# z turned once per half of the rows, and copied to the other half

## The chip, the cores and the metric

One core of one Trainium2 chip runs the kernel. TensorE (PE) does the matmuls and loads their weights (PEld), VectorE (DVE) and ScalarE (ACT) the elementwise work, GpSimd (POOL) and SyncE (SP) issue most DMAs, and 16 DMA engines move the bytes. The time is device microseconds per execution; the median of the runs counts.

## The reference, cut to what matters

```python
# u, v: (8, 3072, 256); z: (8, 3072, 64); float32
scores = (1 / 3072) * np.matmul(z, z.transpose(0, 2, 1))
attn = np.maximum(scores, 0.0) ** 2
x = (u * np.matmul(attn, v)).reshape(8 * 3072, 256)
g = np.maximum(x @ w1, x @ w2)          # w1, w2: 256 x 1024
out = g @ w_out                         # 1024 x 256
```

An attention without softmax over 8 batches, with the scores z zT, followed by a feed-forward layer on all tokens.

## The kernel before

**Tiles.** The 3072 rows of a batch are 24 tiles of 128 rows. Four tiles make a group (g, 512 columns of scores), six groups a batch; two groups are a couple, written (b, c) for batch b, c = 0 to 2. Eight tiles of z or v make a piece, three to a batch. The data are cast to bf16.

**Scores.** z has only 64 columns, so TensorE's 128 rows are used as two halves of 64: `score_pair` (L230) issues two matmuls (L244), one in each half of the rows, which run side by side; half 0 takes the first tile of the pair and half 1 the second. Each reads 64 x 128 weights and 64 x 512 moving columns from `zT`, which holds z turned (features on partitions) for both halves: rows 0 to 63 and rows 64 to 127. `z_at(b, t, half)` (L111) gives the place of a tile in it. There is room for four pieces; piece number 3b + piece goes to slot (3b + piece) mod 4.

**How z gets there.** For batches 2 to 7 `load_z` (L157) loads a piece in bf16 by a DMA from GpSimd; `turn_z` (L163) makes two VectorE copies (L169) that write every tile twice, side by side, into a tile `zd` of 8 x 2 x 64 columns, and one DMA transpose from SP (L170) turns 128 x 1024 elements, so that each tile stands in both halves of the rows. For batch 1 `z_staged` (L151) loads float32 by SP into a free block and GpSimd casts it twice into `zd`. Batch 0 is turned on TensorE.

**Attention.** Relu of the scores goes to a block (128 x 2048, one of 27 in a list that is handed round), its square stays there. The scores are symmetric, so only blocks on and above the diagonal are computed; `mirror` (L287) makes the others by a DMA transpose of 128 x 2048 from SP (L289), and a diagonal block fills its lower triangle by three small ones (L271). From batch 0's last couple on, the product with v is done with seven products in place of eight on sums of blocks (VectorE, L343) and of v (`combine_v`, L193); the matmuls are L1202, 84 steps of two for a couple of batch 1 or later.

**Feed-forward.** `ff_by_seven` (L527) follows for the couple before, and its four results per couple leave by ScalarE copies (L649) and DMAs from SP (L650).

**The order.** Nothing is reordered: every engine and every DMA queue runs its instructions in the order in which the program is written. `at(n, ...)` puts work ahead of step n of a couple; things of one step go in the order of the `at` calls, after the mirrors that became due. In a pass of the loop over couples come the 84 steps of couple (b, c), with the score pairs of what is computed ahead spread among them (at step 2 + n x 82 // N for the n-th of N), then the loads of `loads_behind`, then the feed-forward of the couple before, its output DMAs included. So on SP's queue the four output stores of one pass stand ahead of everything of the next pass's steps. Pairs run ahead: couple (b, 1) computes the last 6 pairs of batch b and the first 8 of batch b + 1, and couple (b, 2) the next 14.

For batch b + 1 the z pieces 0 and 1 are loaded and turned in couple (b, 0) (turned at steps 62 and 74 for b = 1, 44 and 56 for later b) and piece 2 is turned at step 26 of couple (b, 1). Turns of u (`turn_u`, L218, DMA L220) stand at steps 12 and 18 of the couples (b, 1) and (b, 2).

v is loaded by GpSimd (L186) in DMAs of two tiles, 128 KB each, but for batch 0 where they hold four tiles.

Of the kernel before, what the change touches and what calls it, by code (L numbers as in the profile page):

```python
# [12 lines left out]
def kernel(  # L13
# [10 lines left out]
    nc = tc.nc  # L24
    fp32 = mybir.dt.float32
    bf16 = mybir.dt.bfloat16
# [4 lines left out]
    dqk = z.shape[-1]  # L31
    Dff = moe_w1.shape[-1]

    P = 128
    R = 64
    NT = S // P
    G = 4
    GW = G * P
    NG = NT // G
    NC = NG // 2  # L40
# [10 lines left out]
    zpool = ctx.enter_context(tc.tile_pool(name="zpool", bufs=2))  # L51
# [12 lines left out]
    def by_tile(x):  # L64
        return x.rearrange("(p t) d -> p t d", t=NT)
# [39 lines left out]

    zT = zpool.tile([P, 1 + 4 * 2 * G, P], bf16, name="zT", bufs=1)
    zn, zd, z_first, resting = {}, {}, [], []

    def z_at(b, t, half=0):  # L111
        piece, k = divmod(t, 2 * G)
        return 1 + (NC * b + piece) % 4 * 2 * G + k - (half if b == 0 else 0)

    def first_z(lo, n, queue):
        t = hpool.tile([P, n, dqk], fp32, name=f"z32_{lo}", tag="h")
# [19 lines left out]
    def staged(dst, src):  # L136
        home = Block()
        resting.append(home)
        t = home.ap.bitcast(fp32)[:, : dst.shape[1] * dst.shape[2]]
        t = t.rearrange("p (a f) -> p a f", a=dst.shape[1])  # L140
        nc.sync.dma_start(out=t, in_=src)
        return t

    def rested(n):
        for _ in range(n):
            resting.pop(0).release()
# [2 lines left out]
        nc.gpsimd.tensor_copy(dst, staged(dst, src))  # L149

    def z_staged(b, piece):  # L151
        zd[b, piece] = t = zpool.tile([P, 2 * G, 2, dqk], bf16, name="zd")
        t32 = staged(t[:, :, 0, :], by_tile(z[b])[:, ds(piece * 2 * G, 2 * G), :])
        for h in range(2):
            nc.gpsimd.tensor_copy(t[:, :, h, :], t32)

# [4 lines left out]
        )  # L161

    def turn_z(b, piece):  # L163
        if (b, piece) in zd:
            t = zd[b, piece]
        else:
            t = zpool.tile([P, 2 * G, 2, dqk], bf16, name="zd")
            for h in range(2):
                nc.vector.tensor_copy(t[:, :, h, :], zn[b, piece])  # L169
        nc.sync.dma_start_transpose(  # L170
            zT[:, ds(z_at(b, piece * 2 * G), 2 * G), :], t.rearrange("p t h d -> p (t h d)")
        )

# [2 lines left out]
    def load_v(b, piece, lo=0, n=2 * G, held=False):  # L178
        if (b, piece) not in vp:
            vp[b, piece] = vpool.tile([P, 2 * G, D], bf16, name="v_sb")  # L180
        t = vp[b, piece]
        if held:
            nc.vector.memset(t[:, lo, 0:1], 0.0)
        step = 2 if b else n
        for at in range(lo, lo + n, step):
            nc.gpsimd.dma_start(  # L186
                out=t[:, ds(at, step), :], in_=by_tile(v[b])[:, ds(piece * 2 * G + at, step), :]
            )

    def v_at(b, t, dc):  # L190
# [39 lines left out]
    def score_pair(b, g, m, dve_half=None, halves=False, act=False):  # L230
# [9 lines left out]
        for h in range(2):  # L240
            rows = ds(h * R, R)
            q = z_at(b, g * G, h)
            s_ps.append(mm_tile([P, GW], fp32, "s_ps", full=not lo[h])[0])
            nc.tensor.matmul(  # L244
                s_ps[h][:, lo[h] :],
                zT[rows, z_at(b, blk * G + tiles[h], h), :],
                zT[rows, q + lo[h] // P : q + G, :].rearrange("p t c -> p (t c)"),
                start=True,
                stop=True,
            )  # L250
# [600 lines left out]
    def need(b, g, n):  # L851
        most = pair_at[b, g, 2 * g]
        for t in range(n + 1):
            if t // G >= g:
                most = max(most, pair_at[b, g, t // 2] + 1)
        return most

    with tc.manual_schedule():
# [3 lines left out]
        nc.vector.memset(warm[:, :P], 0.0)  # L862
        nc.vector.memset(warm[:, P:], 0.0)
        load_v(0, 0, 0, G)
        make_identity(nc, ident)
        z32.update({lo: first_z(lo, n, nc.gpsimd) for lo, n in ((12, 8), (20, 4))})
        load_v(0, 0, G, G)
        for piece in range(1, NC):
            for lo in (0, G):
                load_v(0, piece, lo, G)  # L870
# [43 lines left out]
        for i in range(PLAIN):  # L914
            b, g = groups[i]
# [5 lines left out]
            for slot, (n, dc) in enumerate(steps_of(i)):  # L921
                k = need(b, g, n)
# [22 lines left out]
                if i in (1, 2) and n in (6, 9):  # L945
                    h = sums[n // 9]
# [21 lines left out]
                if (i, n) in ((1, 15), (2, 14), (3, 4)):  # L968
                    z_staged(1, i - 1)
# [8 lines left out]
                if (i, n) in ((2, 10), (3, 10)):  # L978
                    turn_z(1, i - 2)
                if (i, n) == (3, 16):  # L980
                    turn_z(1, 2)
# [6 lines left out]
                if i == 2 and n in (15, 18):  # L988
                    half = n // 18
# [67 lines left out]
        b, g = groups[PLAIN - 1]  # L1057
# [14 lines left out]
        for i in range(PLAIN // 2, len(couples)):  # L1072
            b, c = couples[i]
            q1, q2 = 2 * c, 2 * c + 1
            if (b, c) == (1, 0):
# [3 lines left out]
                b, c, forms, blocks=() if b else (q2, q1)  # L1079
# [6 lines left out]
            acc, opened, h = {}, {}, {}  # L1086
# [68 lines left out]
            def at(n, do, *args):  # L1155
                events.setdefault(n, []).append(lambda: do(*args))
# [8 lines left out]
                at(18, turn_u, b, q2)  # L1165
            if not b:
                at(20, lambda: rested(len(resting)))
                for n in range(12):
                    at(
                        12 + 7 * n - n // 3 if n < 8 else 21 + 6 * n,  # L1170
                        load_v, 1, (2, 1, 0)[n // 4], 2 * (n % 4), 2,
                    )
            elif b + 1 < B:
                if c == 0:
                    for piece, n in enumerate((24, 30) if b == 1 else (4, 10)):
                        at(n, load_z, b + 1, piece)
                        at((62 if b == 1 else 44) + 12 * piece, turn_z, b + 1, piece)
                    at(80 if b == 1 else 62, load_z, b + 1, 2)
                if c == 1:
                    for n in range(4):  # L1180
                        at(24 + 5 * n, load_v, b + 1, 1, 2 * n, 2)
                    at(26, turn_z, b + 1, 2)

            for s, pair in enumerate(steps):
                tick += 1
# [106 lines left out]
```

## Time and profile before

| | |
|---|---|
| median of 3 runs | 893.77 us (892.32 to 895.35) |
| the profiled execution, in all | 894.84 us |
| its span, first to last instruction | 892.8 us |
| mean granted TensorE clock | 0.999 |
| DMA queue of SP (q1) | 73.9% of 16 engines |
| DMA queue of GpSimd (q0) | 22.6% of 16 engines |
| HBM read, written | 59.77 MB, 25.17 MB |

The profile is that of one execution, in microseconds from the span's start. A row of instructions names the line, the engine, the operation, what it writes and reads, and how many there are; "SPq" is a row of SyncE's queue, whose length is the time that SP takes to issue it, while the landing of a DMA comes later and is listed apart. A DMA issue row such as this one gives count, size and the median time from issue to landing:

```profile
zT<-zd SPq DMA_TRANSPOSE x21, 4.3
v_sb<-in_v_dram POOLq DMA_DIRECT2D x84, 128.0 KB, 6.6
v_sb<-in_v_dram POOLq DMA_DIRECT2D x6, 256.0 KB, 6.2
```

A wait names who waited and for whom, with the sum in us, the number of times and the longest. The share of the DMA engines in a window can go above 1.0, because the packets of one engine overlap.

### The profile page before, as it was taken

The page shows a single profiled execution, that of the slowest core. Times are in us where ns is not written, and L with a number is a line of the kernel's source. Part 1 is how long each engine was busy: PE and PEld are TensorE (multiplying, and loading weights), DVE is VectorE, ACT ScalarE, POOL GpSimd, SP SyncE. Part 2 cuts the span into 40 slices and gives each one's busy share as a digit, 9 for nine tenths or more (in the row PEclk, how much of TensorE's full clock was granted, in tenths as well). Part 3 has the DMA queues.
Part 4 walks back from the last instruction along what each step waited for, and adds up shares of the span by engine and source line. Part 5 has one row for each costly group of instructions (what it writes and reads, how often), then busy time and mean ns, then how long its engine had stood idle before and what let it go on. Part 6 is the DMA issues. An engine that isn't in the chain of part 4 may idle for free.

```text
span 892.8 us, 19566 instructions
## 1 busy us (share of the span) xinstructions
PE 885.2 (99%) x7458; PEld 505.5 (57%) x7458; DVE 764.9 (86%) x1201; ACT 735.4 (82%) x1366; POOL 97.7 (11%) x176
## 2 busy tenths in 40 slices
PE   9999999999999999999999999999999999999997
PEld 4555555565565555655656556566465564655655
DVE  6897887889988899798998899988898889987755
ACT  7978888788888888888888889888889888894554
POOL 3222100111002010020101101011100110000000
PEclk9999999999999999999999999999999999999999
DMA  9999999989899889998999999999989999998302
GB/s 179 250 224 197 201 198 146 205 145 197 168 178 185 175 139 161 191 151 165 173 168 203 153 183 160 149 198 134 212 150 144 189 134 205 144 150 158 80 1 95
DMA packets 396014, 148.10 MB, mean 166 GB/s; under 512 B 361264, under 2 KB 375856, under 8 KB 395920
## 3 DMA queue, kind: packets, MB, share of 16 engines
q1 hardware_dynamic: 373488, 119.32, 73.9%
q0 software_dynamic: 22288, 27.40, 22.6%
q8 instruction: 58, 0.95, 0.4%
q14 instruction: 36, 0.29, 0.1%
q10 hardware_dynamic: 144, 0.13, 0.0%
HBM read 59.77 MB, written 25.17 MB: 95 GB/s over the span
## 4 chain that ended last, share of the span: by engine, by line
PE 98%; DVE 1%; DMA 1%; issue 0%; ACT 0%; DVEq 0%
PE acc L1202 45%; PE acc L552 21%; PE d_ps L607 11%; PE s_ps L244 7%; PE acc L305 4%; PE d_ps L569 4%; PE acc L733 2%; PE d_ps L711 2%; DMA blk<-blk 1%; PE acc L892 0%; PE tpz L129 0%; DVE h_sb L1097 0%; PE w2o_ps L1000 0%; PE acc L675 0%; DVE blk L268 0%
## 5 line engine op out<-in xcount | busy, mean ns | idle before, releaser
L1202 PE MATMUL acc<-blk,v_sb 64*128 64x512 bf16 x2144 | 386.9, 376 | 0.0
L258 ACT ACTIVATE blk<-s_ps 128x512 bf16<-128x512 f32 (+1 forms) x584 | 287.4, 554 | 62.9 <-PE s_ps L244 60.5
L343 DVE TENSOR_TENSOR blk<-blk,blk 128x2048 bf16<-128x2048 bf16 x260 | 313.0, 1220 | 18.4 <-DMA blk<-blk 11.4
L1202 PE MATMUL acc<-blk,vt 64*128 64x512 bf16 x1560 | 316.3, 376 | 0.0
L1202 PEld LDWEIGHTS <-v_sb 64*128 64x128 bf16 x2144 | 152.0, 94 | 126.0 <-issue 5.0
L552 PE MATMUL acc<-w_out_sb,g_sb 128*128 128x256 bf16 x1400 | 190.3, 273 | 0.0
L552 PEld LDWEIGHTS <-g_sb 128*128 128x128 bf16 x1400 | 136.9, 98 | 56.1 <-DVE g_sb L619 0.6
L1202 PEld LDWEIGHTS <-vt 64*128 64x128 bf16 x1560 | 123.8, 94 | 75.5
L582 ACT ACTIVATE g_sb<-d_ps 128x512 bf16<-128x512 f32 x212 | 120.1, 600 | 9.0 <-PE d_ps L607 7.8
L244 PE MATMUL s_ps<-zT 64*128 64x512 bf16 (+3 forms) x672 | 125.5, 357 | 0.5 <-DVE r_sb L256 0.3
L619 DVE CUSTOM_DVE_ANT_0 g_sb<-blk,d_ps 128x512 bf16<-128x512 f32 x133 | 88.7, 684 | 36.4 <-PE d_ps L607 23.7
L268 DVE TENSOR_TENSOR blk<-blk 128x1024 bf16<-128x1024 bf16 x134 | 89.2, 686 | 19.9 <-ACT blk L258 19.9
L266 ACT ACTIVATE blk<-blk 128x1024 bf16<-128x1024 bf16 x78 | 82.3, 1055 | 0.9
L615 ACT COPY blk<-d_ps 128x512 f32<-128x512 f32 x133 | 76.6, 588 | 6.7 <-PE d_ps L607 3.7
L1097 DVE TENSOR_TENSOR h_sb<-h_sb,acc 128x512 f32<-128x512 f32 x89 | 58.9, 684 | 24.0 <-PE acc L1202 16.0
L186 POOL DMA_DIRECT2D v_sb<-in_v_dram x90 | 48.5, 557 | 272.6 <-PE acc L1202 216.5
L607 PE MATMUL d_ps<-blk,wT_sb 128*128 128x512 bf16 x198 | 68.4, 379 | 0.3 <-DVE g_sb L619 0.3
L473 DVE SCALAR_TENSOR_TENSOR xT<-h_sb,uT 128x512 bf16<-128x512 f32 x96 | 61.3, 689 | 2.1 <-DMA uT<-un 2.1
L649 ACT COPY o_sb<-acc 128x512 f32<-128x512 f32 x86 | 48.2, 587 | 14.5 <-PE acc L552 12.0
L244 PEld LDWEIGHTS <-zT 64*128 64x128 bf16 x672 | 35.7, 94 | 37.6 <-issue 0.4
L1101 ACT COPY h_sb<-acc 128x512 f32<-128x512 f32 x66 | 38.9, 590 | 19.3 <-PE acc L1202 17.8
L611 ACT COPY d_ps<-d_ps 128x512 f32<-128x512 f32 x65 | 37.8, 581 | 16.9 <-PE d_ps L607 16.9
(91 smaller groups left out, 782.4 us busy)
## 6 DMA issues: line engine op xcount, KB each, us to landing
out_dram<-o_sb SPq DMA_DIRECT2D x95, 256.0 KB, 3.0
un<-in_u_dram POOLq DMA_DIRECT2D x44, 256.0 KB, 5.3
v_sb<-in_v_dram POOLq DMA_DIRECT2D x84, 128.0 KB, 6.6
blk<-blk SPq DMA_TRANSPOSE x240, 5.1
zn<-in_z_dram POOLq DMA_DIRECT2D x18, 128.0 KB, 4.7
blk<-in_u_dram SPq DMA_DIRECT2D x4, 512.0 KB, 4.5
v_sb<-in_v_dram POOLq DMA_DIRECT2D x6, 256.0 KB, 6.2
blk<-in_moe_w_dram SPq DMA_DIRECT2D x2, 512.0 KB, 4.3
```

The costliest lines, as they stand in the source:

```text
L244: nc.tensor.matmul(s_ps[h][:, lo[h] :], zT[rows, z_at(b, blk * G + tiles[h], h), :], zT[rows, q + lo[h] // P : q + G, :].rearrange("p t c ...
L258: nc.scalar.activation(o, s, AF.Relu)
L266: nc.scalar.activation(both, r, AF.Square)
L268: nc.vector.tensor_mul(both, r, r)
L343: op(*((by_key(x) if mixed else x.ap) for x in blocks))
L473: lambda dc=dc: nc.vector.scalar_tensor_tensor(out=x[:, dc, :].rearrange("p (t r) -> p t r", r=P), in0=hs[dc].rearrange("p (t r) -> p t r" ...
L552: nc.tensor.matmul(o_ps[key][:, t % 2, :], x[:, ts(t, P)], w, start=first, stop=not left[key] and t % 2 == 1, skip_group_check=last,)
L582: nc.scalar.activation(g, ps, AF.Relu)
L607: nc.tensor.matmul(ps, w, x, start=first, stop=ends, skip_group_check=True)
L615: nc.scalar.copy(u_[k, name], ps)
L619: nc.vector._custom_dve(TENSOR_ADD_SAT, out=g, in0=u_[k, with_], in1=ps, s0=float("inf"), s1=0.0)
L1202: mm = nc.tensor.matmul(a.out(acc[name]), w()[rows], a.moving(rows, j), start=first, stop=left[name] == 0, skip_group_check=True,)
```

## The change

Four things change.

- z of batches 2 to 7 is turned once. One VectorE copy makes a tile `zp` of four column groups, each with a tile of the piece's first half (tiles 0 to 3) beside one of its second half (4 to 7), and a DMA transpose of 128 x 512 puts the first four in rows 0 to 63 and the last four in rows 64 to 127. `spread_z` then issues two plain DMAs from SP, each of 64 partitions x 4 tiles (1 KB per partition, 64 KB), that copy to each half the tiles that the other has: one from rows 64 to 127 to rows 0 to 63 four tiles on, one from rows 0 to 63 to rows 64 to 127 four tiles before. `zT` gets 40 tile places in place of 33, and `z_at` moves accordingly.
- The places of `spread_z` in the order: for batches 3 to 7 at steps 64 and 76 of couple (b, 0) for pieces 0 and 1; for batch 2 at steps 6 and 14 of couple (1, 1); piece 2 of each of these batches at step 48 of couple (b, 1).
- z of batch 1 is still turned twice over, but GpSimd casts it into the second half of the block that the load landed in, and these three blocks go back to the list at step 4 of couple (0, 2).
- v of batches 1 to 7 is loaded in DMAs of four tiles (256 KB) in place of two.

```diff
-    zT = zpool.tile([P, 1 + 4 * 2 * G, P], bf16, name="zT", bufs=1)
-    zn, zd, z_first, resting = {}, {}, [], []
+    zT = zpool.tile([P, 5 * 2 * G, P], bf16, name="zT", bufs=1)
+    zn, zd, z_first, z_homes, resting = {}, {}, [], [], []

     def z_at(b, t, half=0):
+        if b == 0:
+            return 1 + t - half
         piece, k = divmod(t, 2 * G)
-        return 1 + (NC * b + piece) % 4 * 2 * G + k - (half if b == 0 else 0)
+        slot = (NC * b + piece) % 4
+        return G * (1 + 2 * slot + slot // 2) + k - (G * half if b > 1 else 0)
...
     def z_staged(b, piece):
-        zd[b, piece] = t = zpool.tile([P, 2 * G, 2, dqk], bf16, name="zd")
-        t32 = staged(t[:, :, 0, :], by_tile(z[b])[:, ds(piece * 2 * G, 2 * G), :])
+        width = 2 * G * 2 * dqk
+        t32 = staged(zT[:, : 2 * G, :dqk], by_tile(z[b])[:, ds(piece * 2 * G, 2 * G), :])
+        z_homes.append(resting.pop())
+        t = z_homes[-1].ap[:, width : 2 * width].rearrange("p (t h d) -> p t h d", h=2, d=dqk)
+        zd[b, piece] = t
...
     def turn_z(b, piece):
+        at = z_at(b, piece * 2 * G)
         if (b, piece) in zd:
             t = zd[b, piece]
         else:
-            t = zpool.tile([P, 2 * G, 2, dqk], bf16, name="zd")
-            for h in range(2):
-                nc.vector.tensor_copy(t[:, :, h, :], zn[b, piece])
+            t = zpool.tile([P, G, 2, dqk], bf16, name="zp")
+            nc.vector.tensor_copy(
+                t, zn[b, piece].rearrange("p (h t) d -> p t h d", h=2)
+            )
         nc.sync.dma_start_transpose(
-            zT[:, ds(z_at(b, piece * 2 * G), 2 * G), :], t.rearrange("p t h d -> p (t h d)")
+            zT[:, ds(at, t.shape[1]), :], t.rearrange("p t h d -> p (t h d)")
         )
+
+    def spread_z(b, piece):
+        at = z_at(b, piece * 2 * G)
+        lo, hi = (zT[ds(h * R, R), ds(at, G), :] for h in range(2))
+        nc.sync.dma_start(out=zT[ds(0, R), ds(at + G, G), :], in_=hi)
+        nc.sync.dma_start(out=zT[ds(R, R), ds(at - G, G), :], in_=lo)
...
-        step = 2 if b else n
-        for at in range(lo, lo + n, step):
+        for at in range(lo, lo + n, G):
             nc.gpsimd.dma_start(
-                out=t[:, ds(at, step), :], in_=by_tile(v[b])[:, ds(piece * 2 * G + at, step), :]
+                out=t[:, ds(at, G), :], in_=by_tile(v[b])[:, ds(piece * 2 * G + at, G), :]
             )
...
                 at(20, lambda: rested(len(resting)))
-                for n in range(12):
-                    at(
-                        12 + 7 * n - n // 3 if n < 8 else 21 + 6 * n,
-                        load_v, 1, (2, 1, 0)[n // 4], 2 * (n % 4), 2,
-                    )
+                at(4, lambda: [home.release() for home in z_homes])
+                for n, step in enumerate((12, 26, 39, 52, 69, 81)):
+                    at(step, load_v, 1, (2, 1, 0)[n // 2], G * (n % 2), G)
             elif b + 1 < B:
                 if c == 0:
                     for piece, n in enumerate((24, 30) if b == 1 else (4, 10)):
                         at(n, load_z, b + 1, piece)
                         at((62 if b == 1 else 44) + 12 * piece, turn_z, b + 1, piece)
+                        if b > 1:
+                            at(64 + 12 * piece, spread_z, b + 1, piece)
                     at(80 if b == 1 else 62, load_z, b + 1, 2)
                 if c == 1:
-                    for n in range(4):
-                        at(24 + 5 * n, load_v, b + 1, 1, 2 * n, 2)
+                    for n in range(2):
+                        at(24 + 10 * n, load_v, b + 1, 1, G * n, G)
                     at(26, turn_z, b + 1, 2)
+                    at(48, spread_z, b + 1, 2)
+                    if b == 1:
+                        for piece in range(2):
+                            at(6 + 8 * piece, spread_z, b + 1, piece)
```

## The prediction

> **What bounds the kernel now.** I read the page first, parts 1 and 4.
>
> ```profile
> span 892.8 us, 19566 instructions
> PE 885.2 (99%) x7458; PEld 505.5 (57%) x7458; DVE 764.9 (86%) x1201; ACT 735.4 (82%) x1366; POOL 97.7 (11%) x176
> ...
> PE 98%; DVE 1%; DMA 1%; issue 0%; ACT 0%; DVEq 0%
> ```
>
> TensorE is busy for 885.2 of 892.8 us and holds 98% of the chain that ended last. Work saved on another engine shows only where TensorE waits for it. So the second view is TensorE's own waits from 60 us to the end:
>
> ```profile
> PE d_ps L607 <- DVE g_sb L619: 1.5, 2, 1.2
> PE s_ps L244 <- DVE r_sb L256: 0.3, 1, 0.3
> ```
>
> That is all that a faster VectorE or a freer DMA could give back: 1.8 us. The 1.5 us sit at 147 to 151 us, where VectorE waited for a mirrored block that landed late (in the chain, "DMA blk<-blk" for 4.83 us from 141.94).
>
> The change lives on SP's queue and the DMA engines, so the third view is SP's timeline in the couple (1,1):
>
> ```profile
> 148.10 1.85 SPq L170 DMA_TRANSPOSE zT<-zd  x1
> ...
> 155.24 1.29 SPq L170 DMA_TRANSPOSE zT<-zd  x1
> 156.62 1.28 SPq L220 DMA_TRANSPOSE uT<-un  x1
> 158.00 4.80 SPq L289 DMA_TRANSPOSE blk<-blk  x1
> 162.90 2.09 SPq L650 DMA_DIRECT2D out_dram<-o_sb  x4
> 165.09 2.60 SPq L220 DMA_TRANSPOSE uT<-un  x1
> 167.86 5.34 SPq L289 DMA_TRANSPOSE blk<-blk  x1
> 173.29 1.26 SPq L220 DMA_TRANSPOSE uT<-un  x1
> ```
>
> Each row starts where the one before ends: SP has no idle time here and runs behind. How far behind is seen from the data of the four output stores: ScalarE wrote the last of it at 156.21 + 1.24 = 157.45 us, and SP issues the first store at 162.90.
>
> **The change, part by part.**
>
> *z of batches 3 to 7 (and piece 2 of batch 2).* Per piece, one VectorE copy instead of two: the row L169 has 286 ns for a 512-column copy, so 18 x 0.29 = 5.1 us less VectorE. Worth nothing: TensorE's only waits for VectorE are the two above, which lie before all but three of these copies. On SP the turn halves to 512 columns, but the issue hardly does: L170 takes 1.287 us for 1024 columns, L271 1.201 us for 384 to 128, so 0.09 us saved. Two copies are added. No SBUF to SBUF copy is in the trace; the nearest rows are the output stores L650, 0.406 us of issue each, or 2.09 / 4 = 0.52 with the gaps. Per piece SP is busy 2 x 0.52 - 0.09 = 0.95 us longer, 2.9 us per batch of some 108 us. SP waits on many rows and catches up in every stretch of the feed-forward, so I cost this at nothing; without that cover the blocks behind it come 0.95 us later per piece. The tightest of these pieces is piece 2 of batch 4: the slot of its copies is at 399.0 us, just ahead of a mirror, they land at 406 to 408, and TensorE's first use is at 409.2. That holds, with 1 to 3 us to spare. For pieces 0 and 1 of batch 3 (slots at 256.7 and at latest 266.4, uses at 273.85 and 282.4) there are some 10 us. Each copy also waits on SP for its turn to have landed (median 4.3 us after issue). Twenty steps lie between, over 4 us, and the turn itself is ahead in the same queue, so this wait is nothing while SP lags; without the lag, 1 us of SP time, which then has room.
>
> *v loads.* Outside batch 0, 84 loads of 128 KB become 42 of 256 KB. GpSimd saves 42 x 0.557 = 23.4 us of issue that nobody waits for. Landing: 6.6 us for 128 KB, 6.2 for 256 KB, so no later. Nothing; the cover is the feed-forward that follows, and without it half a microsecond per batch either way.
>
> *The blocks that hold z of batch 1.* GpSimd casts into the second half of the staging block, and three blocks of 27 go back at step 4 of the couple (0,2): two of them later than before, one earlier than step 20. No instruction is added. I cost it at nothing, with the 1.8 us of TensorE's known waits as its bound above and below, since it can only move mirrors of that stretch.
>
> *z of batch 2, pieces 0 and 1: the price.* Here the copies are put at steps 6 and 14 of the couple (1,1). In SP's order step 6 stands behind the four stores L650 and ahead of turn_u of step 12, which is the row at 165.09. Step 14 stands behind the mirror of step 13, ahead of the row at 173.29. When does TensorE need them? The couple has 14 score pairs (28 matmuls L244), the n-th at step 2 + n x 82 // 14; the first six finish batch 1, the seventh, at step 37, is batch 2's first. It needs both copies, since each half of the rows reads the other's tiles. In TensorE's timeline the seventh stands here, and the thirteenth, the first with piece 1, below it:
>
> ```profile
> 165.74 0.38 PE L244 MATMUL s_ps<-zT 64*128 64x512 bf16 x2
> ...
> 174.26 0.38 PE L244 MATMUL s_ps<-zT 64*128 64x512 bf16 x2
> ```
>
> So the score matmul that needs the copies comes 0.65 us after SP so much as reaches their slot. Step by step: the slot at 165.09; less what the two halved turns ahead of it give back. SP's issue alone would give 2 x 0.09 = 0.2 us. The DMA engines would give 2 x 0.9: queue q1's 373,488 packets hold 73.9% of 16 engines for 892.8 us, 28 ns each, and 512 of them over 16 engines are 0.9 us. The engines are full here (share 1.16 from 143 to 160 us), so I take 1.3. First copy at 163.8, second at 163.8 + 0.52 = 164.3. Its landing goes by the rows that stand directly ahead of it in the queue:
>
> ```profile
> out_dram<-o_sb SPq DMA_DIRECT2D x4, 256.0 KB, 5.6
> ...
> blk<-blk SPq DMA_TRANSPOSE x2, 8.0
> ```
>
> (the window 156 to 172 us). From below: 2.0, the fastest L650 of the kernel; from above: 8.0, the mirrors of this window. I take 5.6, as the copy queues behind those very stores: 169.9. TensorE then stands still from 165.74 to 169.9, **4.2 us**. Queued behind that matmul is all of TensorE's program; ScalarE and VectorE wait for it and nothing runs on, so it is added whole. The second piece: slot 173.29 - 1.3 + 0.52 x 2 = 173.0 for the first copy, 173.5 for the second, landed some 5 us later (uT's turns, its neighbours there, take 4.0 over the kernel and 5.8 in that window), at 178.5. Needed at 174.26 + 4.2 = 178.5, so it adds about nothing; alone it would cost as much as the first.
>
> The Trainium skill, "DMA: Bandwidth & Descriptors", section "Anatomy of one DMA — SWDGE (gpsimd) path", gives a DMA about 2.0 us plus its bytes at 436 GB/s; it fits that on GpSimd's path. For a 64 KB copy that is an estimated 2.15 us, and the sum would come to 0.7 us of waiting. No trace so far shows such a copy; the L650 rows of this window, 5.6 us, are above that figure.
>
> **Sum.** 892.8 + 4.2 = 897.0 us of span. That execution took 894.84 in all, 1.07 above the median of the runs, 893.77; on the median the forecast is 893.77 + 4.2 = **898.0 us**.
>
> **Rivals.**
> 1. *SP has caught up (not slower).* If the slow stretch of DMA at 159 to 161 us (63, 38 and 21 GB/s in the window's slices) does not recur, the stores go out at 157.5, as their data come, take 2.09, and the copies follow at 159.6 and 160.1. They land 3.0 to 5.6 us later, by 165.7, and TensorE waits for nothing. It decides once SP reaches the slot before 165.74 - 5.6 - 0.52 = 159.6. For it: the runs differ by 3 us, so such stretches come and go. Against: SP's rows have no gap from 143 us on. Time 893.8, or 892.0 with all 1.8 us won back; I write 893.3. Chance 0.25.
> 2. *The copies do not queue.* They land at the 2.0 us of the fastest store: 166.3, a wait of 0.6, 894.4 us. For it: L650's median over the kernel is 3.0, so where nothing is queued a transfer is back soon, and a copy carries a quarter of a store's bytes. Against: the stores just ahead took 5.6. The Trainium skill's figure above would put it here. Chance 0.12.
> 3. *Nothing is given back and both pieces are late.* Copies at 165.1 and 165.6, landed 8.0 later at 173.6: 7.9 us. The second piece from 173.29 + 1.04 + 0.52 = 174.9, landed at 182.9, against 174.26: 8.6 us in all, 902.4. For it: 8.0 is the mirrors' own row in this window. Chance 0.08.
> 4. *The freed DMA time is worth more than the waits show.* Halved turns and longer v packets would have to quicken TensorE itself by over 2.7 us; part 4 shows 98% TensorE and no wait left to fill. 890.5 us. Chance 0.07.
>
> **How the numbers follow.** The forecast has 0.48. About 0.3%, 2.7 us, is what a measurement of this kernel tells from no change. Slower by more: forecast and rival 3, 0.56. Within: rivals 1 and 2, 0.37. Faster: rival 4, 0.07. The forecast's own range runs from a landing of 4.1 us to the full 8.0 without relief, 2.7 to 7.9 us, so 896.5 to 901.7. The range for 8 in 10 goes on to rivals 1 and 2 below (892.0, less 0.3 for the runs' spread, 891.7) and to rival 3 above, 902.4.
>
> **What would show it.** In the profile after: a TensorE wait at L244 for "DMA zT<-zT" near 166 us, about 4 us long, and none like it in batches 3 to 7; SP's copies right behind four L650 rows; L170 at about 1.2 us. Wrong: no such wait (rival 1, if the stores go out by 158; rival 2, if they still go out late), or L244 waiting in later batches, which would say that SP's 2.9 us per batch has no cover.

## The result, and the profile after

The kernel after takes **906.14 us** (median of 5 runs, 904.56 to 908.50) against 893.77 before (5 runs, 892.32 to 897.82). The ratio is 1.0126, with a 95% interval of 1.0097 to 1.0155: 1.3% slower. The forecast was 898.0, the upper end of its range 902.4. Ratios, here and below, leave out executions that took over 1.5% longer than the fastest of the same kernel; medians and ranges are of all. The profiled execution has a span of 904.4 us, 11.6 more than before.

The head of the page and its chain of waits, after:

```profile
span 904.4 us, 19530 instructions
...
PE 889.1 (98%) x7458; PEld 512.3 (57%) x7458; DVE 761.4 (84%) x1183; ACT 736.0 (81%) x1366; POOL 74.9 (8%) x134
...
PE 93%; DMA 4%; DVE 2%; issue 1%; ACT 0%; SPq 0%; DVEq 0%; POOLq 0%
```

Before, TensorE was busy for 885.2 of 892.8 us, so 7.6 idle; now it is 889.1 of 904.4, so 15.3 idle. The 11.6 us are 7.7 more of idle time and 3.9 more of "busy" time for the same 7458 matmuls. The second number can't be a wait: the matmuls themselves have become longer somewhere. DMA has gone from 1% of the chain to 4%.

TensorE's waits after (sum, times, longest):

```profile
PE s_ps L257 <- DMA zT<-zT: 7.3, 1, 7.3
PE acc L1219 <- DVE h_sb L1110: 2.0, 2, 1.4
...
PE acc L1219 <- DVE blk L356: 0.8, 1, 0.8
```

One wait for the copies (L257 is the score matmul, L244 before), a single time, and none in batches 3 to 7. The two lower rows lie between 90 and 140 us; before had none of this size there.

SP's queue around the couple (1,1), after. Start, length of the issue, line (L178 the turn of z, L233 of u, L302 the mirror, L663 the stores, L185 and L186 the copies):

```profile
159.78 1.26 SPq L233 DMA_TRANSPOSE uT<-un  x1
161.14 4.99 SPq L302 DMA_TRANSPOSE blk<-blk  x1
166.22 2.06 SPq L663 DMA_DIRECT2D out_dram<-o_sb  x4
168.33 0.54 SPq L185 DMA_DIRECT2D zT<-zT  x1
168.92 0.58 SPq L186 DMA_DIRECT2D zT<-zT  x1
```

The order is that of before, with the copies directly behind the four stores. The next two views are TensorE's first score matmul of batch 2, with the idle time ahead of it, and the windows before it, during the wait, behind it and after that (length; busy us of PE, PEld, DVE, ACT and POOL; granted clock; DMA share; GB/s):

```profile
175.68 0.86 PE L257 MATMUL s_ps<-zT 64*128 64x512 bf16 x2 [7.28 <-DMA zT<-zT]
```

```profile
160.00:168.00 8.00, 8.00 (x79) 5.16 (x76) 6.24 (x11) 6.54 (x14) 2.11 (x4) 1.00 0.95 156
168.00:175.60 7.60, 0.40 (x4) 0.00 (x0) 3.58 (x8) 0.59 (x1) 0.00 (x0) 0.86 1.12 262
175.60:180.20 4.60, 4.52 (x22) 3.02 (x24) 1.42 (x2) 3.03 (x5) 0.00 (x0) 0.50 0.99 207
180.20:189.00 8.80, 8.80 (x87) 7.29 (x85) 6.22 (x16) 5.38 (x14) 2.12 (x4) 1.00 0.48 80
```

The first copy was issued at 168.33, TensorE stopped at 168.4 (175.68 - 7.28), and the matmul ran at 175.68: from issue to use 7.3 us. Behind the wait the granted clock is 0.50 for 4.6 us, which takes another 4.6 x 0.50 = 2.3 us. A pair of score matmuls shows it too: 0.86 us here, 0.38 before the change. So the one stall costs 7.3 + 2.3 = 9.6 of the 11.6 us; the waits of 2.0 and 0.8 us between 90 and 140 us are the next part, and 1.5 us of before's wait at 147 us are gone.

What stood ahead of the copies shows in the stores' row of the window 156 to 172 us (5.6 before, in the prediction) and in the packets of two stretches, 168.3 to 173.5 and 173.5 to 175.7 us. A copy moves 1 KB packets, a store and a load here 2 KB, a transpose 256 bytes:

```profile
out_dram<-o_sb SPq DMA_DIRECT2D x4, 256.0 KB, 7.3
```

```profile
DMA packets 796, 1.40 MB, mean 269 GB/s; under 512 B 120, under 2 KB 120, under 8 KB 795
...
q0 software_dynamic: 338, 0.59, 65.5%
q1 hardware_dynamic: 457, 0.79, 42.3%
```

```profile
DMA packets 940, 0.55 MB, mean 251 GB/s; under 512 B 685, under 2 KB 813, under 8 KB 940
```

In the first stretch no packet lies between 512 bytes and 2 KB: both copies had been issued by 169.5 us, and until 173.5 none of their packets had started. In the second there are 813 - 685 = 128, all of both copies. So the copies did stand behind the stores in SP's queue for most of their 7 us, and the stores took 7.3 us to land, with GpSimd's loads (q0) holding 65.5% of the engines' time beside them.

Where the loss ends shows in TensorE's rows. Here is the same group near the end, before and then after:

```profile
879.66 0.60 PE L552 MATMUL acc<-w_out_sb,g_sb 128*128 128x256 bf16 x4
```

```profile
891.90 0.60 PE L565 MATMUL acc<-w_out_sb,g_sb 128*128 128x256 bf16 x4
```

TensorE reached batch 2's first score 2.7 us later than before (168.4 against 165.74). At batch 3's first score it is 12.3 us behind (286.17 against 273.85) and here 12.2, so in this execution nothing is lost after the stall.

### The profile page after: what moved, and what is told of

The parts are those of the page before. It is cut to its first block, busy times and chain, and to the rows that moved or that the text cites. A ratio compares the mean times of both kernels' runs of the same rounds, so it can differ in the third digit from the quotient of the medians.

```text
span 904.4 us, 19530 instructions
## 1 busy us (share of the span) xinstructions
PE 889.1 (98%) x7458; PEld 512.3 (57%) x7458; DVE 761.4 (84%) x1183; ACT 736.0 (81%) x1366; POOL 74.9 (8%) x134
## 4 chain that ended last, share of the span: by engine, by line
PE 93%; DMA 4%; DVE 2%; issue 1%; ACT 0%; SPq 0%; DVEq 0%; POOLq 0%
PE acc L1219 43%; PE acc L565 21%; PE d_ps L620 11%; PE s_ps L257 7%; PE acc L318 5%; PE d_ps L582 4%; DMA blk<-blk 2%; PE acc L746 1%; DVE blk L356 1%; DMA zT<-zT 1%; PE d_ps L724 1%; DMA v_sb<-in_v_dram 1%; PE w2o_ps L1013 0%; DVE blk L277 0%; PE acc L688 0%
## 5 line engine op out<-in xcount | busy, mean ns | idle before, releaser
L257 PE MATMUL s_ps<-zT 64*128 64x512 bf16 (+3 forms) x672 | 129.7, 359 | 7.3 <-DMA zT<-zT 7.3
L257 PEld LDWEIGHTS <-zT 64*128 64x128 bf16 x672 | 37.5, 94 | 45.8 <-DMA zT<-zT 7.9
L565 PE MATMUL acc<-W2o_sb,xT 128*128 128x256 bf16 x344 | 51.6, 273 | 0.0
```

The source lines that it names most:

```text
L257: nc.tensor.matmul(s_ps[h][:, lo[h] :], zT[rows, z_at(b, blk * G + tiles[h], h), :], zT[rows, q + lo[h] // P : q + G, :].rearrange("p t c ...
L565: nc.tensor.matmul(o_ps[key][:, t % 2, :], x[:, ts(t, P)], w, start=first, stop=not left[key] and t % 2 == 1, skip_group_check=last,)
```

## The experiments

The runs of before that stand beside the experiments have medians of 894.0 to 895.1 us. Ratios are to these, with 95% intervals. "Steps" are those of the couple.

**1. The copies early.** The kernel after, with the copies of batch 2's pieces 0 and 1 at the end of couple (1,0)'s steps, ahead of the mirror and the stores.

```diff
+            if (b, c) == (1, 0):
+                for piece in range(2):
+                    spread_z(2, piece)
...
-                    if b == 1:
-                        for piece in range(2):
-                            at(6 + 8 * piece, spread_z, b + 1, piece)
```

> The changed kernel, but the copies of batch 2's pieces 0 and 1 stand at the end of couple (1,0)'s steps, ahead of the mirror and the four output stores of that pass. Theory (the copies queue behind the stores): they land by 166 us, the 7.3 us wait of TensorE for zT is gone and the slow pace after it (1.5 us) with it: 906.1 - 8.8 = 897.3. Rival, the wait only moves (stores and mirrors behind them late): over 900.

Measured: **896.50 us** (12 runs, 891.88 to 906.75), 1.0012 [0.999, 1.0035]. TensorE's waits:

```profile
PE acc L565 <- DVE g_sb L632: 5.1, 2, 3.3
PE acc L1216 <- DVE blk L356: 2.7, 1, 2.7
```

No wait for the copies is left; they landed 4.1 to 5.0 us after issue. Moving four instructions gives back some 10 of the 12 us, so the place of these copies is the main loss. The two waits shown are others; the profiled execution was the longest of the twelve, so they speak of its own excess over the median, not of the median.

**2. The copies behind the mirror, ahead of the stores.**

```diff
+                if (b, c) == (0, 2) and token == "E0":
+                    for piece in range(2):
+                        spread_z(2, piece)
```

> The changed kernel, but batch 2's four copies stand behind the mirror and ahead of the four output stores of the same pass: only the order of copies and stores is exchanged. In the profile after, the mirror issued at 161.14 landed at 169.46, the stores from 172.77 to 175.37 and the first two copies at 175.63 and 175.89, one behind the other. Theory, first come first served in SP's queue: the copies land 0.3 to 0.6 us behind the mirror, at about 170, TensorE waits some 2 us, the clock does not drop, and the time is 906.1 - 5.3 - 2.3 = 898.5. Rival, a copy takes 7 us from its issue in this stretch whatever stands ahead of it: landed at 173.3, a wait of 5 us, 903 to 904.

Measured: 901.01 us (10 runs, 892.72 to 903.06), 1.0067 [1.0044, 1.009]. The first row is TensorE's wait; behind it stands SP's queue:

```profile
PE s_ps L257 <- DMA zT<-zT: 4.6, 2, 2.8
```

```profile
159.77 5.14 SPq L302 DMA_TRANSPOSE blk<-blk  x1
165.00 0.55 SPq L185 DMA_DIRECT2D zT<-zT  x1
165.61 0.58 SPq L186 DMA_DIRECT2D zT<-zT  x1
```

The copies are issued 3.3 us earlier than in the kernel after, and the wait shrinks by 2.7 us. But with no store ahead of them they still land 5.2 us (at 170.2) and 6.8 us (at 172.4) after issue, while GpSimd's loads hold 88.9% of the engines' time (165.6 to 170.2 us): taking the stores away does not make the landing short. The clock behind this wait was 0.61 for 4.4 us. The time lies between the expected 898.5 and the rival's 903.

**3. The copies from ScalarE's queue**, at the same steps.

```diff
-                            at(6 + 8 * piece, spread_z, b + 1, piece)
+                            at(6 + 8 * piece, spread_z, b + 1, piece, nc.scalar)
```

> The changed kernel with those four copies issued from ScalarE's queue in place of SP's, at the same steps 6 and 14. If the copies were late because they stood in SP's queue behind a mirror and four stores: issued at about 161 us, landed 2 to 3 us later, no wait, 897.3. If the 16 DMA engines are simply full: landed 5 to 7 us after the issue, by 168, a wait of 0 to 2 us, 897 to 900, and the landing tells it.

Measured: 905.69 us (6 runs, 895.23 to 915.18), 1.0098 [1.006, 1.0136]. ScalarE's timeline, in the longest of these executions:

```profile
157.77 0.51 ACTq L185 DMA_DIRECT2D zT<-zT  x1
...
170.78 0.47 ACTq L185 DMA_DIRECT2D zT<-zT  x1
172.30 0.47 ACTq L186 DMA_DIRECT2D zT<-zT  x1
172.81 1.43 ACT L271 ACTIVATE blk<-s_ps 128x128 bf16<-128x128 f32 x4 [9.21 <-DMA out_dram<-o_sb]
```

The first piece's copies, issued at 157.77 and 160.19 with nothing ahead in their own queue, land at 163.0 and 167.0, after 5.3 and 6.8 us (DMA share 0.89 and 1.09 in these stretches). With run 2 that makes 5 to 7 us for a 64 KB copy from either queue. The run can't price the copies themselves: the second piece's issue was held until 170.8. What held it is open: the view puts ScalarE's 9.2 us of idle time down to SP's stores, whose data these copies neither read nor write. TensorE then waited 7.9 us for ScalarE's relu. In this execution a DMA put on a computing engine's queue held that engine.

**4. TensorE kept busy during the wait.** The kernel after, with 34 matmuls of 128 x 512 ahead of batch 2's first score, into a PSUM bank that this score then overwrites.

```diff
+            if (b, g, m, h) == (2, 0, 2, 0):
+                for _ in range(34):
+                    nc.tensor.matmul(
+                        s_ps[0], w15_sb[:, 0, :P], w15_sb[:, 0, :GW], start=True, stop=True
+                    )
```

> The changed kernel; ahead of batch 2's first score matmul TensorE multiplies 34 times 128x512 (7.3 us at the full clock) into the same bank of PSUM, which the score matmul then starts anew, so the product is thrown away. The wait for the copies is filled with work, nothing else is moved. In the profile after, the granted clock is 0.50 from 175.6 to 180.2 us, right behind 7.3 us of waiting. Theory, the idle time itself drops the clock: the copies land as before, the granted clock stays 1.00 behind them, and the time is 906.1 - 2.3 = 903.8. Rival, the slow stretch has another cause (DMA traffic, weight loads): clock 0.5 there again and 906.1.

Measured: 900.87 us (8 runs), 1.0087 [1.0055, 1.012]. Five of the runs lie at 900.1 to 901.5 and three at 907.3 to 908.7. TensorE's timeline and two windows:

```profile
167.35 7.51 PE L259 MATMUL s_ps<-w_sb 128*128 128x512 bf16 x33
174.79 0.39 PE L262 MATMUL s_ps<-zT 64*128 64x512 bf16 x2
```

```profile
172.00:176.00 4.00, 4.00 (x26) 1.68 (x25) 0.00 (x0) 0.79 (x2) 0.00 (x0) 1.00 1.28 212
176.00:180.00 4.00, 4.00 (x42) 2.14 (x38) 3.63 (x5) 3.75 (x8) 0.00 (x0) 1.00 0.64 127
```

The copies, issued at 166.00 and 166.71, are as late as ever (landed 7.0 and 7.1 us after issue, the last at 173.8), but the clock stays at 1.00 and the pair of scores takes 0.39 us, not 0.86. The score stands right behind the added matmuls, some 1 us after the last copy. So idle time, not the transfers, brought the half clock. What this is worth in time is less clear: the windows give 2.3 us less that 1 us, the medians 5.3 us, but these come from different sets of runs, and the ratios' intervals overlap (1.0087 to 1.0126, or 3.5 us).

**5. v by two tiles in the kernel after**, at the steps of before, everything else as changed.

```diff
-        for at in range(lo, lo + n, G):
+        step = 2 if b else n
+        for at in range(lo, lo + n, step):
...
-                    for n in range(2):
-                        at(24 + 10 * n, load_v, b + 1, 1, G * n, G)
+                    for n in range(4):
+                        at(24 + 5 * n, load_v, b + 1, 1, 2 * n, 2)
```

> The kernel after, with v loaded by two tiles as before, and everything else as changed: the late copies of batch 2 stay where they are. Theory (the late copies and the clock behind their wait are the loss, v loads cost some 2.5 us on their own and do not set the slot): the wait for zT at batch 2's first score pair stays between 6 and 8 us, the half clock behind it too, and the median falls from 906.1 to 903 to 904.5 us. Rival A (the 256 KB loads are what kept the queue behind, so that the relief of 1.3 us did not come and the copies took 7 us to land): the slot comes at 166 to 167 us, the wait shrinks to 3 to 5 us, the clock hardly drops, and the median is 897 to 900 us. Rival B (v has nothing to do with it): 906 us, wait as after.

Measured: 903.77 us (6 runs, 901.90 to 908.74), 1.0117 [1.0087, 1.0147]. TensorE's wait, SP's queue and the window behind the wait:

```profile
PE s_ps L258 <- DMA zT<-zT: 7.6, 1, 7.6
```

```profile
162.38 2.28 SPq L664 DMA_DIRECT2D out_dram<-o_sb  x4
164.71 0.66 SPq L185 DMA_DIRECT2D zT<-zT  x1
165.42 0.84 SPq L186 DMA_DIRECT2D zT<-zT  x1
```

```profile
172.40:177.00 4.60, 4.59 (x28) 3.22 (x30) 1.47 (x2) 3.17 (x5) 0.00 (x0) 0.64 1.04 216
```

The whole wait is there without the long v loads. This execution had no wait over 0.3 us between 90 and 140 us, so it compares closely with before: TensorE wants the copies at 164.84 (172.41 - 7.57; before 165.74), the slot is at 164.71 (before 165.09), so it is 0.13 us ahead of the need where it was 0.65, and the copies land 7.7 and 7.2 us after issue.

**6. v loads alone**: before, with the loads of four tiles for all batches; then for batch 1 only; then for batches 2 to 7 only. The steps are those of the change. The line that differs, in this order:

```diff
-        step = 2 if b else n
+        step = G
...
+        step = 2 if b > 1 else n
...
+        step = G if b > 1 else 2 if b else n
```

> The kernel before with the v loads of four tiles alone. The time is 12.4 us longer after the change, and the forecast had 4.2, so some 4 us sit elsewhere: in the profile after, TensorE waits for VectorE at 92 to 138 us, and two mirrors there take 14 and 11.5 us to land while 256 KB loads of v are in flight. Theory A, the larger loads hold the mirrors: 893.8 + 3 to 4 = 897 to 898, with mirrors over 10 us to landing between 95 and 115 us and TensorE waits by 140 us. Rival, the held blocks or chance: 892.5 to 895.

> The kernel before with four-tile loads for v of batch 1 alone (six loads in couple (0,2)). The v loads alone came out at 1.0028. Theory, the cost lies here, where mirrors and loads meet and VectorE waits for mirrors: 1.002 to 1.004, 895.5 to 898. Rival, it lies in the later batches: 1.000, 893 to 895.

> The kernel before with four-tile loads for v of batches 2 to 7 alone. Theory, the cost lies in couple (0,2): no change here, 893 to 895. Rival, each batch pays a little, or a triangle comes late now and then: 895.5 to 898.

Measured: 897.22 us (1.0028 [1.0009, 1.0048]) for all; 897.92 (1.0037 [1.0016, 1.0057]) for batch 1; 897.53 (1.0029 [1.0005, 1.0053]) for the others, 12 runs each. Each is slower by some 2.5 to 3.3 us, and the parts don't add up to the whole, so the intervals are too wide to divide it; that the cost lies in couple (0,2) alone is not borne out. TensorE's largest waits in the first:

```profile
PE acc L1198 <- DVE h_sb L1096: 1.4, 1, 1.4
PE acc L551 <- DVE g_sb L618: 1.1, 1, 1.1
```

The first stands between 85 and 165 us, as the like-named one in the kernel after, and between 105 and 122 us VectorE waited 2.07 and 3.36 us for mirrors (2.32 and 4.05 in the kernel after, a single 2.55 in before). But single waits as long stand there with v of batch 1 by two tiles too: 3.70 us in run 5, 3.85 in the third run here, 4.67 in run 8; and in batch 1's own run the profiled execution had none. That larger loads hold the mirrors is not shown. It stays open.

**7. The held blocks alone**: before, with batch 1's z cast in its staging block.

```diff
-        zd[b, piece] = t = zpool.tile([P, 2 * G, 2, dqk], bf16, name="zd")
+        z_homes.append(resting.pop())
+        t = z_homes[-1].ap[:, width : 2 * width].rearrange("p (t h d) -> p t h d", h=2, d=dqk)
+        zd[b, piece] = t
...
+                at(4, lambda: [home.release() for home in z_homes])
```

> The kernel before with z of batch 1 cast inside its staging block, and the three blocks given back at step 4 of couple (0,2), alone. Theory A (the larger v loads are what costs the early 4 us): no change, 892.5 to 895. Rival, the held blocks delay or reorder the mirrors: 896 to 898, with the VectorE wait at 78 us longer than the 4.8 us of before.

Measured: 895.24 us (12 runs), 1.0006 [0.9993, 1.002]: nothing.

**8. The early copies with v by two tiles** (the edits of 1 and 5 together).

> The kernel spread_early (batch 2's copies ahead of the stores) with v loaded by two tiles as before: what remains is z turned once, its copies and the held blocks. spread_early came out at 1.0012 of before, v loads alone at 1.0028. Theory A, the larger v loads cost 1 to 2.5 us wherever they are: 893 to 894.5, and no VectorE wait for a mirror over 3 us between 105 and 125 us. Rival, the remaining microsecond is the copies' SP time: no change, 895 to 897.

Measured: 897.47 us (12 runs, 892.66 to 904.70), 1.0018 [0.9993, 1.0043]. No gain over run 1, within both intervals, against the 893 to 894.5 of theory A: the 2.5 us of run 6 do not show when they are taken back here, and no version found beats the kernel before.

**9. No copies for batch 2's first two pieces**: each is turned twice over, in two parts, through the tiles `zp`, as before the change; then the same with v by two tiles.

```diff
+        if b == 2 and piece < 2:
+            for part in range(2):
+                t = zpool.tile([P, G, 2, dqk], bf16, name="zp")
+                for h in range(2):
+                    nc.vector.tensor_copy(t[:, :, h, :], zn[b, piece][:, ds(part * G, G), :])
...
+            return
```

> The changed kernel, but pieces 0 and 1 of batch 2 are turned twice over, as before the change (in two DMAs of four tiles each), and get no copies. If all of the 7.3 us wait and the 2.3 us behind it come from these two pieces' copies: as spread_early, 894.5 to 897.5, no wait for zT. Rival, the place of the copies matters only in part and other pieces' copies cost as well: over 899.

> wide2 with v loaded by two tiles: z of batches 3 to 7 turned once and nothing else that was found to cost. If SP's 2.9 us more per batch is hidden, as the forecast had it: 893 to 895.5, the time of before. If it is not: over 896, with VectorE waits for triangles (L284) in couples (b, 1) of the later batches and TensorE waiting behind them.

Measured: 907.04 us (1.0132 [1.0107, 1.0157]) and 908.66 (1.0118 [1.0078, 1.0158]). Both failed as tests, by a wait of the edit's own. VectorE in the first:

```profile
148.39 0.36 DVE L175 COPY zp<-zn 128x256 bf16<-128x256 bf16 x2 [8.76 <-DMA zT<-zp]
```

There are two `zp` tiles; the third part waits for the first turn to land, and TensorE waits 8.5 us for VectorE. They say nothing on the copies, but they show a stall's price once more: from 148 to 157 us, the last of this wait and what follows it, the granted clock is 0.54.

**10. The later copies doubled.** The kernel of run 1, with each copy of batches 3 to 7 issued a second time.

```diff
+        for n in range(2 if b > 2 else 1):
```

> spread_early with every copy of batches 3 to 7 issued twice, so that SP has 15 x 2 more DMAs of 64 KB, some 2.9 us more per batch. If that SP time is hidden, as the forecast costed it: as spread_early, 1.0012 of before or 895 to 897. If it is what makes spread_early's runs spread from 892 to 907: 899 to 903, with TensorE waits behind late triangles in couples (b, 1).

Measured: 932.11 us (6 runs), 1.0406 [1.0382, 1.043]. SP's queue at 417 us:

```profile
418.15 0.58 SPq L187 DMA_DIRECT2D zT<-zT  x1
424.60 0.46 SPq L186 DMA_DIRECT2D zT<-zT  x1
```

SP stands for 5.9 us, since the repeat writes the place of the first copy and waits for it to land. So this doubled a wait as well as SP's time, and another run was needed. The profile has a short wait of TensorE, though, that says something of the clock: 2.1 us at 193.2, and the clock behind it.

```profile
193.20:195.30 2.10, 0.03 (x1) 0.03 (x2) 1.91 (x3) 0.44 (x1) 0.00 (x0) 1.00 1.05 233
195.30:199.70 4.40, 4.40 (x24) 2.03 (x26) 2.85 (x4) 2.03 (x4) 0.00 (x0) 0.61 0.24 49
```

**11. The later copies doubled, without that wait**: the extra copies go to places of `zT` that hold nothing by then.

```diff
+        if b > 2:
+            odd = (NC * b + piece) % 2
+            nc.sync.dma_start(out=zT[ds(0, R), ds(5 * G * odd, G), :], in_=hi)
+            nc.sync.dma_start(out=zT[ds(R, R), ds((4 + 5 * odd) * G, G), :], in_=lo)
```

> The copies of batch 2 at the end of couple (1,0), as in the earlier run with them there (896.5 us), and for each piece of batches 3 to 7 two more copies of 64 KB that nobody reads, into places of zT that hold nothing by then, so that no added copy waits for another one to land. This doubles the copies' time on SP (some 1.2 us more per piece, 3.6 us per batch) without the waits that the run with repeated copies had. Theory (SP's time in batches 3 to 7 has cover, as forecast; the 35 us of the repeated copies came from the waits between them): the same as without them, 895 to 898 us, and no wait of TensorE over 1.5 us from 240 us on. Rival (SP's time there is not covered, the mirrors and triangles behind the copies come late): each of five batches loses 1 to 4 us and the clock behind the wait, 903 to 918 us, with waits for g_sb in the couples (b, 1).

Measured: 908.21 us (median of 6; five lie at 903.1 to 910.0, the sixth took 1028.0 at a mean clock of 0.851), 1.0138 [1.0108, 1.0169], some 11 us above run 1. TensorE's wait, VectorE's just before it, and the window behind:

```profile
PE acc L569 <- DVE g_sb L636: 6.3, 2, 5.8
```

```profile
416.29 1.23 DVE L360 TENSOR_TENSOR blk<-blk,blk 128x2048 bf16<-128x2048 bf16 x1 [6.98 <-DMA blk<-blk]
```

```profile
419.50:424.00 4.50, 4.50 (x23) 1.88 (x23) 2.09 (x4) 2.26 (x4) 0.00 (x0) 0.50 0.27 55
```

The rival of this expectation held, though not as it was drawn: not 1 to 4 us in each of five batches, but one stall in the couple (3,1), where VectorE waits for a block's triangle, with half clock behind it. Not all of the 11 us is the added copies': this profile also has a wait of 2.6 us at 123 us with a clock of 0.63 behind it, ahead of any of them, as run 1's longest execution had.

The triangle landed at 416.26, where VectorE could have gone on at 409.3. In the profile of before the triangle at this place lands at 404.11 and is used at 404.61: half a microsecond of cover (and in run 6 with batch 1's loads alone VectorE waits 1.17 us for it, with no copies at all). The added copies take the DMA engines as well as SP, and the run doesn't part the two.

Of the kernels with the copies of the change, the profiled executions of run 3 (VectorE 7.3 us) and run 4 (VectorE 4.8 us, TensorE 3.6) have the same stall, while the kernel after, run 5 and run 8 have none there. That the plain copies cause it isn't shown: in run 4 one mirror ahead of the triangle took SP 8.89 us to issue (at 390.65), against 5.49 in the kernel after and 5.28 in before. That run 4's three runs at 907 to 909 are such executions fits, since the profiled one is among them (908.11), but the other two weren't profiled.

## Why the prediction was right or wrong, step by step

**The bound, the place and the sign: right.** TensorE's one new long wait is at the score matmul for zT, near 166 us forecast and at 168.4 measured, right behind the four stores, once, with none in later batches. Run 1 shows by a move of four instructions that it is the main loss. Rivals 1 and 2 (SP caught up; no queueing) and 4 fell. Rival 3's first half came true: nothing given back, and a landing near its 8.0, so 7.9 us of waiting against the measured 7.3; its second piece added nothing, as the forecast had it. With the wait as measured the forecast would have been 893.8 + 7.3 = 901.1 us; what took the time past 902.4 is the clock and the stretch ahead of the wait, below.

**"so I take 1.3": failed, by some 2 us.** The relief of two halved turns was to bring the slot to 163.8, 1.95 us ahead of the need. In the kernel after the slot stood 0.07 us ahead of it (168.33 against 168.4), in run 5 0.13, in run 4 1.35 (166.00 against 167.35). In run 5, which compares best, the slot moved by 0.4 us only (165.09 to 164.71), and the need moved ahead by 0.9 (165.74 to 164.84); before's 1.5 us wait at 147 us is not in that execution. Whether freed DMA time took that wait away isn't shown: it is also missing in the profiles of runs 6 and 7, which turn z as before, and run 4 has one of 1.5 us at 149. Run 5 shows that the v loads are not what kept the queue behind.

**"I take 5.6": the reason held, the size was too small, by 1.4 to 2.1 us.** Measured 7.3, 7.0 (after), 7.7, 7.2 (run 5), 7.0, 7.1 (run 4). The copy does queue behind those very stores, as forecast, and landed as they did; but the stores took 7.3 us in the kernel after, 5.6 in before. The upper bound that the forecast named, 8.0, was nearer. Runs 2 and 3 show 5.2 to 6.8 us with no store ahead, so the queue is not all of it: GpSimd's loads fill much of the engines there. No run moved the loads away.

**"nothing runs on, so it is added whole": missed a term of 2.3 us.** The wait was costed as its own length. TensorE then ran at half clock for 4.6 us. The Trainium skill, "TensorE: Matmul & The Clock Gate", section "Part 1: The HAM clock gate (the "warmup" mystery)", states that an idle window of about 3.4 us takes the clock to one half, and that some 3.4 us of sustained work bring it back. The trace agrees: 0.50 behind 7.3 us of idle time, and 1.00 from 180.2 us on; run 4 takes the idle time away, and the drop is gone with it. With the forecast's own wait of 4.2 us this rule would already have applied. The runs also show the drop behind waits well below that figure, 2.1 us in run 10 and 2.6 in run 11, and none behind 1.5 us (run 4, clock 1.00 to 154 us); here the measurement decides. Behind 3.6 us of waiting in run 4 the clock was 0.60 for 4 us, so 1.6 us; with 1.6 to 2.3 added the forecast would have been 899.6 to 900.3.

**v loads "nothing": too small, but inside the named bound.** Alone they cost 1.0028 [1.0009, 1.0048], some 2.5 us; the bound of half a microsecond per batch makes 3.5 us for seven batches. Landing times alone (6.9 us for 256 KB after, 6.6 for 128 KB before) did not show it. In company with the late copies their part can't be told from nothing: 1.0126 with them, 1.0117 without.

**The held blocks "nothing": right** (run 7).

**The copies of batches 3 to 7 "nothing": right in the profile of after, but near an edge.** TensorE's distance to before does not grow there after the stall (12.3 us at batch 3's first score, 12.2 near the end). The forecast feared for piece 2 of batch 4 at its own use. What is tight there is the triangle's use by VectorE at 404.61, 0.5 us, and doubling the copies falls over that edge (run 11).

Put together for the profiled execution: TensorE comes to the wait 2.7 us late, then 7.3 us of wait and 2.3 of clock in place of 4.2 make the 12.3 us that stay to the end (the span, with what follows TensorE, ends 11.6 us later). Of the 2.7 us, the early waits of 2.8 less before's 1.5 explain about half; their cause stays open (runs 6 and 8), and for the rest no row can be named.

## What to carry to other kernels

Before work is put behind others on a queue that runs behind, compare its slot with the need, and price the landing by the slowest neighbour of that stretch; a slot that is late can sometimes just be moved, as the four instructions of run 1, which gave back some 10 us. A stall of the engine that bounds the kernel costs its length and the clock behind it, and here waits of 2.1 us and more cost 1.6 to 2.9 us on top of their length (runs 2, 4, 5, 10, 11 and the kernel after). A step that costs "nothing" has a margin: look for the smallest one behind it on its queue, not only for its own.

## What the runs showed of the hardware

- The clock drops behind waits shorter than the one forecast here: 3.6 us in run 4 at 416 us (0.60 for 4 us), 2.6 us in run 11 at 123 us (0.63 for 4.6 us), 2.1 us in run 10 at 193 us (0.61 for 4.4 us). What it takes follows the wait's length only loosely: 2.3 us behind 7.3 (after), 4.6 x 0.36 = 1.7 behind 7.6 (run 5), 5.8 x 0.50 = 2.9 behind 5.8 (run 11).
- A 64 KB copy within SBUF landed 5.2 to 7.7 us after issue with stores or loads in flight ahead of or beside it, 4.1 to 5.0 in run 1, and 2.1 in the kernel after (issued 176.83, landed 178.92), 8 us later in the same couple, with neither beside it, though the DMA share was 0.95 there. Neither its size nor that share alone says how long it takes.
- SP needs 0.54 to 0.59 us to issue such a copy, near the forecast's 0.52, and 1.2 us for the turn of 512 columns against 1.29 for 1024: halving a transpose saves SP next to nothing.
